# Half of the first expert's first layer moved into the first batch's attention, with new due times

## The chip, the cores and the metric

The kernel runs on one core of a Trainium2 chip. The metric is the device time of one execution in microseconds, as a median over runs. The engines are TensorE (PE; its weight loads have a row of their own, PEld), VectorE (DVE), ScalarE (ACT), GpSimd (POOL) and SyncE (SP), which here only issues DMAs. Each engine works through its own queue in order and waits on semaphores for the others.

## The reference

Attention over pooled queries, then two feed-forward networks, everything in fp32. B = 2 batches, H = 8 heads, 1152 keys, 576 pooled queries, head size 64; the model width is 512.

```python
q_pool = q.reshape(B, H, S // 2, 2, D).mean(axis=3)
scores = q_pool @ k.T / sqrt(D)
attn = exp(scores - max(scores)); attn = attn / (attn.sum() + 1e-9)
x = (attn @ v), as [1152, 512]
p = domain_probs / (domain_probs.sum(-1) + 1e-9)
out = sum over 4 experts e of p[:, e] * (relu(x @ w1[e]) @ w2[e])      # 512 -> 1024 -> 512
g = out @ w_gate
result = (g * sigmoid(g) * (out @ w_val)) @ w_out                      # 512 -> 1536 -> 512
```

## The kernel before, in words

**Attention** is cut into 32 units u: batch, pair of heads, half of the queries (288 of them), head within the pair. Units 0 to 15 are batch 0, 16 to 31 batch 1. A unit has nine chunks of 128 keys. Its steps are: `scores` (two chunks into one pair of PSUM banks, two products of 128x288 for each chunk, L503 and L504), `copy_scores` (ACT, L520, the bank into the SBUF tile `s`), `max_scores` (DVE, L527 to L531, a running maximum `acc`), `turn_max` (PE transposes `acc`, tile `mt`, L537), `reduce_max` (DVE, `top`, L547), `spread_max` (PE, `m`, L559), `copy_max` (ACT, L569), `subtract` (three groups of three chunks, L576: group 0 on DVE, groups 1 and 2 on POOL), `expo` (ACT, L582), `av` (PE, L609, the product with the values), `take_part`, `invert`, `scale` (ACT, DVE, POOL: numerator over denominator into `xst`) and `split_x` (L360, L363). Transposes of keys and queries (`prep_k`, `prep_q`, tile `tr`, L447 and L473) stand between them. In batch 0 `av` is an fp32 product, which takes two PE instructions; nearly everything else splits an fp32 number into a high and a low half and makes three products (hi·hi, hi·lo, lo·hi) in their place. In batch 1 the exponentials are split too (`half_hi`, `half_lo`, L587 and L594).

**PSUM** in this part has three pairs of banks p0, p1, p2 and two single banks c and d. Scores go round p0, p1, p2. Bank c holds the `av` sums. All transposes, `mt` and `m` share bank d, so each of them waits until the one before has been read.

**Experts** (`experts`, L873): for each batch and expert eight column blocks f of layer 1, each a sum over four 128-row chunks c of x (chunk c holds heads 2c and 2c+1) for both halves s of the queries, 24 matmuls of 128x288; then layer 2, also 192 matmuls. Blocks go to p0 and p1 in turn; `evict_h` (ACT, L914) and `evict_h2` (DVE, L918) empty one. Weights come in pieces of 256 KB (`load_piece`, three buffers) and are split by `split_hi` (ACT, L315) and `split_lo` (L322; for batch 0's odd pieces POOL, else DVE). Batch 0's experts run between the steps of batch 1's attention, batch 1's experts after it, and then the gated network (tile `g`, then `o`).

**Order.** Nobody writes the order of attention and batch 0's experts by hand. Each step is given to a planner with a due time, an engine, a cost and the names that it reads, writes and holds (`at`). `Plan.arrange` then goes through the engines and on each picks, of the steps that are ready, the one with the earliest due time. So a table of due times sets every queue's order, and on the chip the queues then run as fast as their waits allow. Unit u's steps are due at 9u plus a number for each kind of step; the experts' products are due at

```python
total = experts(0, at, lambda n: E0_START + n / E0_RATE)
```

with n a count of matmuls.

Of the kernel before, what the change touches and what calls it, by code (L numbers as in the profile page):

```python
# [21 lines left out]
TOP = (1.875 - 2.0**-23) * 2.0**-96  # L22
# [4 lines left out]
MT, TOP, MB, MCOPY = 10.23, 11.11, 11.18, 12.05  # L27
SUB = (11.07, 10.75, 13.58)
EXP = ((13.43, 16.94, 15.82), (12.68, 14.5, 17.57))
HALF_HI = (14.41, 16.21, 16.25)  # L30
HALF_LO = (13.1, 15.0, 17.1)
AV = (17.93, 15.5)
FINISH = (22.33, 24.2)
SHARE = (0.7, 2.54, 2.4, 3.2, 3.7)
COPY, MAX = 0.94, 0.25
PREP_Q, PREP_K = (4.3, 5.58, 0.4), (6.33, -0.27)
SPLIT = (-9.69, -6)
E0_START = 159.71
E0_RATE = 9.69
LAST = 18  # L40
# [123 lines left out]
def tile_kernel(  # L164
# [14 lines left out]
    P = 128  # L179
# [72 lines left out]
    def columns(w, c0, c1, o):  # L252
        return w[c0 * P : c1 * P, o * P : (o + 1) * P].rearrange("(c p) o -> p c o", p=P)
# [31 lines left out]
    def narrow(i, words):  # L285
# [6 lines left out]
            up, words[:, :, 1].bitcast(F32), DOWN, TOP, op0=ALU.mult, op1=ALU.min  # L292
        )
        nc.vector.tensor_scalar_max(up, up, -TOP)
# [211 lines left out]
    def score_bank(u, c):  # L506
        return "p2" if u >= LAST else f"p{(u * (KC + 1) // 2 + c // 2) % 3}"
# [137 lines left out]
    def plan_attention():  # L645
        def due_k(jj, g, t, bank):
# [5 lines left out]
            for i in range(2):  # L652
                at(
                    t + PREP_K[1], "ACT", 0.48, prep_k_half, jj, g, i, False,
                    reads=[("ptk", jj, g)], writes=[("kth", jj, i, g)],
# [3 lines left out]
                    t + PREP_K[1], "DVE", 0.555, prep_k_half, jj, g, i, True,  # L659
# [4 lines left out]
        def due_q(u, t, bank):  # L664
# [6 lines left out]
                t + PREP_Q[2], "ACT", 0.41, prep_q_hi, u,  # L671
# [3 lines left out]
                t + PREP_Q[2], "DVE", 0.45, prep_q_lo, u,  # L675
# [31 lines left out]
        for u in range(B * UPB):  # L707
            t = KC * u
            b, jj, half, i = where(u)
            r = 2 * half + i  # L710
            for c in range(0, KC, 2):
# [11 lines left out]
                    t + c + COPY, "ACT", 0.65 if n == 2 else 0.41, copy_scores, u, c,  # L723
                    reads=[("sc", u, c)],
                    writes=[("s", u, c + m) for m in range(n)],
                    **{"uses" if c else "takes": [("S", u) if c else ("s", ("S", u))]},
                )
                if c:
                    at(
                        t + c + MAX, "DVE", 0.75 if n == 2 else 0.92,  # L730
# [7 lines left out]
                t + MT, "PE", 0.25, turn_max, u, kind="f",  # L738
# [3 lines left out]
                t + TOP, "DVE", 0.555, reduce_max, u,  # L742
# [3 lines left out]
                t + MB, "PE", 0.2, spread_max, u, kind="f",  # L746
# [3 lines left out]
                t + MCOPY, "ACT", 0.41, copy_max, u,  # L750
                reads=[("m", u)], writes=[("mc", u)], takes=[("m", ("mc", u))],
            )
            for g in range(3):
                chunks = range(3 * g, 3 * g + 3)
                at(
                    t + SUB[g], "POOL" if g else "DVE", 2.05 if g else 1.05, subtract, u, g,
# [5 lines left out]
                    t + EXP[b][g], "ACT", 0.925, expo, u, g,  # L762
                    writes=[("s", u, c) for c in chunks], uses=[("S", u)],
                )
                if b:
                    at(
                        t + HALF_HI[g], "ACT", 0.925, half_hi, u, g,
# [4 lines left out]
                        t + HALF_LO[g], "POOL" if g else "DVE", 2.05 if g else 1.05, half_lo, u, g,  # L772
# [6 lines left out]
                for cs in [chunks] if b == 0 else [[c] for c in chunks]:  # L779
                    at(  # L780
                        t + AV[b] + cs[0], "PE", 1.46 if b == 0 else 0.397, av, u, cs,
# [8 lines left out]
            end = t + FINISH[b]  # L790
            p = u // 2
            for n in range(2):
# [3 lines left out]
                    reads=[("av", u)], writes=[(tag, p, i)], takes=[] if i else [(tag, (tag, p, 2))],  # L796
                    uses=[(tag, p, 2)],
                )
            if i == 1:
                for n in range(2):  # L800
                    at(
                        end + SHARE[n], "DVE", 1.02, invert, u, n,
# [4 lines left out]
                    end + SHARE[2], "POOL", 0.85, scale, u, kind="port",  # L807
# [76 lines left out]

    def experts(b, at, due):

        pbs, hs, pss, yts = {}, {}, {}, {}
        n = 0
        w = b * PER_BATCH

# [301 lines left out]
```

## Time and profile before

| | |
|---|---|
| time, three runs | median 919.43 us (918.15 to 921.57) |
| the profiled execution | span 920.0 us from the first instruction to the last; the page gives it no other time |
| PE busy, PEld busy | 890.4 us (97%), 845.9 us (92%) |
| DVE, ACT, POOL busy | 575.9, 462.0, 387.7 us |
| chain that ended last | 87% PE |

A row of the profile's stretches has, for each engine, its busy time in that stretch and the count of its instructions. PE counts a matmul as busy from its issue to its modelled end, so that several overlap; PEld counts weight loads, one for each matmul. PEclk is the clock that TensorE was granted, as a share of 2.4 GHz; 0.50 is 1.2 GHz.

### The profile page before, as it was taken

To read this page: it belongs to the slowest core of one execution; us is meant where nothing else is said; L and a number is where in the kernel's file an instruction comes from. 1 tells how busy PE (TensorE), PEld (TensorE's weight loads), DVE (VectorE), ACT (ScalarE), POOL (GpSimd) and SP (SyncE) were. 2 spreads that over 40 slices of the span, in tenths; PEclk is the share of its full clock that TensorE was granted. 3 is DMA by queue.
4 is the path that set the end of the run, shared out by engine and by line. 5 is a ranking of instruction groups with operands and counts; after the bars stand their busy time and mean duration, and the time that the engine had idled before them with its cause. 6 is when DMAs were issued, how large, how long until landed. Compare 5 with 4: busy or idle time off the path is not lost.

```text
span 920.0 us, 14980 instructions
## 1 busy us (share of the span) xinstructions
PE 890.4 (97%) x5916; PEld 845.9 (92%) x5916; DVE 575.9 (63%) x883; ACT 462.0 (50%) x786; POOL 387.7 (42%) x266
## 2 busy tenths in 40 slices
PE   5898989999999999999999999999999999999998
PEld 4777767899999999999999999999999999999886
DVE  5678877766667577675654334333468988888800
ACT  5678868877777677666633223232323333333110
POOL 4456566767776796778631000203023332222000
PEclk9999999999999999999999999999999999999999
DMA  5031121323233223112243232323333322223210
GB/s 141 1 78 39 41 74 51 87 73 86 66 89 87 70 73 83 46 59 60 58 149 94 87 100 81 94 83 89 94 93 96 111 69 92 92 75 101 78 69 34
DMA packets 124149, 72.30 MB, mean 79 GB/s; under 512 B 32304, under 2 KB 119344, under 8 KB 124080
## 3 DMA queue, kind: packets, MB, share of 16 engines
q1 hardware_dynamic: 124080, 71.36, 26.8%
q8 instruction: 46, 0.75, 0.3%
q14 instruction: 23, 0.19, 0.1%
HBM read 68.96 MB, written 2.38 MB: 78 GB/s over the span
## 4 chain that ended last, share of the span: by engine, by line
PE 87%; DVE 5%; ACT 4%; POOL 2%; issue 2%; DMA 0%; SPq 0%; DVEq 0%; POOLq 0%; ACTq 0%
PE ps L873 43%; PE g L873 16%; PE av L609 11%; PE o L873 8%; PE sc L503 3%; PE sc L504 3%; DVE acc L531 1%; ACT s L520 1%; POOL s L576 1%; ACT s L582 1%; PE mt L537 1%; PE tr L447 1%; PE tr L473 1%; ACT kt L463 1%; DVE kt L465 1%
## 5 line engine op out<-in xcount | busy, mean ns | idle before, releaser
L315 ACT ACTIVATE whi<-wraw 128x512 fp32r<-128x512 f32 x128 | 80.6, 630 | 172.5 <-PE ps L873 153.8
L576 POOL TENSOR_TENSOR s<-s,m 128x864 f32<-128x864 f32 x64 | 132.1, 2084 | 78.5 <-ACT m L569 78.4
L873 PE MATMUL ps<-xhi,whi 128*128 128x288 f32 x512 | 153.0, 299 | 0.0
L873 PE MATMUL ps<-hhi,whi 128*128 128x288 f32 x512 | 152.2, 297 | 0.0
L873 PE MATMUL ps<-hhi,wlo 128*128 128x288 f32 x512 | 151.0, 295 | 0.0
L873 PE MATMUL ps<-xhi,wlo 128*128 128x288 f32 x512 | 151.0, 295 | 0.0
L873 PE MATMUL ps<-hlo,whi 128*128 128x288 f32 x512 | 150.9, 295 | 0.0
L873 PE MATMUL ps<-xlo,whi 128*128 128x288 f32 x512 | 150.9, 295 | 0.0
L322 DVE TENSOR_TENSOR wlo<-wraw,whi 128x512 fp32r<-128x512 f32 x96 | 80.2, 835 | 102.1 <-ACT whi L315 101.9
L940 POOL TENSOR_TENSOR yacc<-yacc,yt 128x576 f32<-128x576 f32 x24 | 41.3, 1723 | 187.8 <-DVE yt L934 187.8
L520 ACT ACTIVATE s<-sc 128x576 f32<-128x576 f32 (+1 forms) x160 | 93.2, 601 | 52.2 <-PE sc L504 50.7
L582 ACT ACTIVATE s<-s 128x864 f32<-128x864 f32 x96 | 87.6, 920 | 20.0 <-DVE s L576 15.0
L873 PE MATMUL g<-yhi,wlo 128*128 128x384 f32 x288 | 96.3, 334 | 0.5 <-DVE wlo L322 0.5
L873 PE MATMUL g<-yhi,whi 128*128 128x384 f32 x288 | 96.2, 334 | 0.5 <-ACT yhi L1031 0.5
L873 PE MATMUL g<-ylo,whi 128*128 128x384 f32 x288 | 96.2, 334 | 0.0
L873 PEld LDWEIGHTS ps<-xlo,whi 128*128 128x128 f32 x512 | 96.2, 188 | 0.0
L873 PEld LDWEIGHTS ps<-hlo,whi 128*128 128x128 f32 x512 | 96.1, 188 | 0.0
L873 PEld LDWEIGHTS ps<-xhi,whi 128*128 128x128 f32 x512 | 96.1, 188 | 0.0
L873 PEld LDWEIGHTS ps<-hhi,whi 128*128 128x128 f32 x512 | 96.1, 188 | 0.0
L873 PEld LDWEIGHTS ps<-xhi,wlo 128*128 128x128 f32 x512 | 96.1, 188 | 0.0
L873 PEld LDWEIGHTS ps<-hhi,wlo 128*128 128x128 f32 x512 | 96.1, 188 | 0.0
L503 PE MATMUL sc<-qhi,kt 128*128 128x288 f32 x288 | 88.8, 324 | 5.9 <-DVE acc L531 2.8
(94 smaller groups left out, 1957.8 us busy)
## 6 DMA issues: line engine op xcount, KB each, us to landing
wraw<-in_moe_w_dram SPq DMA_DIRECT2D x128, 256.0 KB, 2.7
w<-in_moe_w_gate_dram SPq DMA_DIRECT2D x12, 512.0 KB, 3.7
w<-in_moe_w_val_dram SPq DMA_DIRECT2D x12, 512.0 KB, 3.7
w<-in_moe_w_out_dram SPq DMA_DIRECT2D x12, 512.0 KB, 3.5
qraw<-in_q_dram SPq DMA_DIRECT2D x32, 144.0 KB, 2.3
kraw<-in_k_dram SPq DMA_DIRECT2D x14, 288.0 KB, 3.7
v<-in_v_dram SPq DMA_DIRECT2D x8, 288.0 KB, 4.0
vraw<-in_v_dram SPq DMA_DIRECT2D x8, 288.0 KB, 3.0
```

What stands on the lines that cost most here:

```text
L315: nc.scalar.activation(out=hi, in_=t, func=AF.Copy)
L322: eng.tensor_tensor(out=lo, in0=t, in1=hi.bitcast(F32), op=ALU.subtract)
L447: nc.tensor.matmul(pt[:, m * P : (m + 1) * P], kr[:, c].rearrange("p h d -> p (h d)"), ident, is_transpose=True,)
L463: nc.scalar.activation(out=kt[me, sl], in_=pt[me, : 3 * P], func=AF.Copy)
L503: nc.tensor.matmul(ps, wt, qhi, start=True, stop=False)
L504: nc.tensor.matmul(ps, wt, qlo, start=False, stop=True)
L520: nc.scalar.activation(out=s[:, c : c + n, :], in_=ps[:, :n, :W], func=AF.Copy)
L576: eng.tensor_tensor(out=sg, in0=sg, in1=m.unsqueeze(1).to_broadcast([P, 3, W]), op=ALU.subtract)
L582: nc.scalar.activation(out=sg, in_=sg, func=AF.Exp)
L609: nc.tensor.matmul(avs[u][:, :W], w[:, c].rearrange("p t d -> p (t d)"), e, start=(c == 0 and n == 0), stop=(c == KC - 1 and n == len(term ...
L873: nc.tensor.matmul(ps, w, x, start=first and n == 0, stop=last and n == len(terms) - 1)
L940: nc.gpsimd.tensor_tensor(out=y, in0=y, in1=yts[o], op=ALU.add)
```

## The change

For expert 0 of batch 0 layer 1 is made in two parts. **Early part**: chunks c = 0 and 1 of x, heads 0 to 3, 12 matmuls for each of the eight blocks, 96 in all. They are due from 96.12 on at 1.625 matmuls per unit of time, within batch 0's attention. They go to bank pair p1, and `evict_early` copies each block out as fp32 (even blocks ACT, odd ones DVE) into a tile that `hlo` will use later. From unit 8 on scores therefore use only p0 and p2. **Late part**: chunks 2 and 3, the other 96 matmuls, where the whole block stood; then `add_early` (DVE) adds the saved sum in PSUM, and `evict_h` and `evict_h2` follow as before. The weight pieces of this layer are cut anew: two chunks by two blocks, so that pieces 0 to 3 serve the early part and 4 to 7 the late one; their number and size stay. Three of these are loaded about 54 units of time sooner.

The due times become a table `DUE` with three numbers for each kind of step: units 0 to 7, units 8 to 15, and batch 1. Three extra dependencies keep the planner's bookkeeping right. `TOP` is renamed to `LIMIT` where it is a number (that code runs for other input types only).

```diff
...
-MT, TOP, MB, MCOPY = 10.23, 11.11, 11.18, 12.05
-COPY, MAX = 0.94, 0.25
...
+DUE = {
+    "mt": (4.55, 8.38, 4.08),
...
+    "copy": (-0.74, -7.74, -2.17),
...
+SPLIT = (0.43, 2.72)
+EARLY_SPLIT = (4.47, 17.53)
+E0_START = 161.44
+E0_RATE = 10.078
+E00_START = 96.12
+E00_RATE = 1.625
+EARLY = 8
+LAST = 17
...
-    for _ in range(B):
+    for b in range(B):
         for e in range(NE):
-            pieces += [columns(w1[e], 0, MC, f) for f in range(FC1)]
+            if b or e:
+                pieces += [columns(w1[e], 0, MC, f) for f in range(FC1)]
+            else:
+                for c in range(0, MC, 2):
+                    pieces += [columns(w1[e], c, c + 2, f, 2) for f in range(0, FC1, 2)]
             for o in range(MC):
...
     def score_bank(u, c):
-        return "p2" if u >= LAST else f"p{(u * (KC + 1) // 2 + c // 2) % 3}"
+        n = u * (KC + 1) // 2 + c // 2
+        return "p2" if u >= LAST else f"p{n % 2 * 2}" if u >= EARLY else f"p{n % 3}"
...
+        def during(u):
+            phase = 2 if u >= UPB else u // (UPB // 2)
+            return {name: times[phase] for name, times in DUE.items()}
...
+        def evict_early(f):
+            early[f] = hp.tile([P, SQ], F32, tag="hlo", name=f"part{f}")
+            out, ps = two(early[f]), pss[0, f, "early"][:, :, :W]
+            if f % 2:
+                nc.vector.tensor_copy(out=out, in_=ps)
+            else:
+                nc.scalar.activation(out=out, in_=ps, func=AF.Copy)
+
+        def add_early(f):
+            ps = pss[0, f][:, :, :W]
+            nc.vector.tensor_tensor(out=ps, in0=ps, in1=two(early[f]), op=ALU.add)
 
...
         def expert_bank(group):
-            return f"p{(group[0] * (FC1 + MC) + group[1]) % 2}"
+            return "p1" if len(group) == 3 else f"p{(group[0] * (FC1 + MC) + group[1]) % 2}"
...
+        if b == 0:
+            m = 0
+            for f in range(FC1):
+                group = (0, f, "early")
+                ps = ("ps", b, *group)
+                for s in range(NH):
+                    for c in range(2):
+                        hidden_product(
+                            due_early(m), group, ps, w, c, f % 2 * P, s, c, c == 0, c == 1
+                        )
+                        m += 3
+                    if f % 2 == 0 and s == 1:
+                        due_split(w + 1, due_early(m) + EARLY_SPLIT[0], due_early(m) + EARLY_SPLIT[1])
+                at(
+                    due_early(m - 1) + 0.1, ("ACT", "DVE")[f % 2], (0.64, 0.755)[f % 2],
+                    evict_early, f,
+                    reads=[(*ps, 0), (*ps, 1)], writes=[("part", f)], uses=[ps],
+                    takes=[("hlo", ("part", f))],
+                )
+                w += f % 2
+
...
+                late = b == 0 and e == 0 and hidden
+                    for c in range(2, MC) if late else range(MC):
+                        if late:
+                            hidden_product(
+                                due(n), group, ps, w, c - 2, f % 2 * P, s, c, c == 2, c == MC - 1
+                            )
...
+                    if s == (1 if late else 0) and not (late and f % 2):
+                        due_split(w + 1, due(n) + SPLIT[0], due(n) + SPLIT[1])
+                w += f % 2 if late else 1
+                if late:
+                    at(
+                        due(n - 1) + 0.3, "DVE", 0.76, add_early, f,
+                        reads=[("part", f)], writes=[(*ps, 0), (*ps, 1)], uses=[ps],
+                    )
...
         for n in range(3):
-            due_load(n, 130 + n)
-        due_split(0, E0_START - 4, E0_START - 3)
+            due_load(n, E00_START - 20 + n)
```

The order of the queues, before and after, at three places. First PE's queue where unit 0's maximum has been spread (tile m) and its exponentials are awaited; sc are scores, tr transposes of queries (qraw) or keys (kraw), av the products with the values. Before:

```order
L559 MATMUL m<-ident,top_235 128x96 x3
L473 MATMUL tr<-ident,qraw_96 128x96 x3
L609 MATMUL av<-s_176,v_102 128x288 x3
L473 MATMUL tr<-ident,qraw_96 128x96 x3
L503 MATMUL sc<-qhi_263,kt_131 128x288
L504 MATMUL sc<-qlo_270,kt_131 128x288
```

Now the row of m is followed by twelve score matmuls of unit 2, one transposition of queries and four more score matmuls of unit 2; the last two of these stand first here:

```order
L538 MATMUL sc<-qhi_212,kt_131 128x288
L539 MATMUL sc<-qlo_214,kt_131 128x288
L645 MATMUL av<-s_176,v_102 128x288 x3
L482 MATMUL tr<-ident,kraw_157 128x128 x3
L645 MATMUL av<-s_176,v_102 128x288 x6
L573 MATMUL mt<-ident,acc_235 96x128 x3
```

Sixteen score matmuls of unit 2 now stand ahead of unit 0's first av, where there were none; the other transposition of queries has gone ahead of unit 1's scores.

Second, PE's queue behind unit 10's m, two thirds through batch 0. Before:

```order
L609 MATMUL av<-s_883,v_104 128x288 x3
L537 MATMUL mt<-ident,acc_1013 96x128 x3
L609 MATMUL av<-s_883,v_104 128x288 x3
L559 MATMUL m<-ident,top_1117 128x96 x3
L503 MATMUL sc<-qhi_967,kt_652 128x288
L504 MATMUL sc<-qlo_974,kt_652 128x288
L473 MATMUL tr<-ident,qraw_964 128x96 x3
L609 MATMUL av<-s_980,v_102 128x288 x6
L473 MATMUL tr<-ident,qraw_964 128x96 x3
```

Now (m stands six rows ahead of the first one here, with a group of av and two chunks' scores between; ps<-xhi and so on are early products, of which twelve follow in a row up to the second transposition):

```order
L538 MATMUL sc<-qhi_993,kt_649 128x288
L539 MATMUL sc<-qlo_1003,kt_649 128x288
L645 MATMUL av<-s_908,v_104 128x288 x3
L508 MATMUL tr<-ident,qraw_990 128x96 x3
L918 MATMUL ps<-xhi_496,whi_869 128x288
L918 MATMUL ps<-xlo_497,whi_869 128x288
L918 MATMUL ps<-xhi_496,wlo_870 128x288
```

Between m and the transposition of queries, where one chunk's scores stood, there are now three chunks' scores and two groups of av, and behind it early products.

Third, DVE's queue where the first expert starts (hlo is `evict_h2`, el `half_lo`, s `subtract`, acc the maximum, den the denominator, wlo `split_lo`, top `reduce_max`). Before:

```order
L531 TENSOR_TENSOR acc_1826<-sc,s_1766 128x576
L322 TENSOR_TENSOR wlo_1829<-wraw_1304,whi_1828 128x512
L918 SCALAR_TENSOR_TENSOR hlo<-ps,hhi 128x576 x2
L576 TENSOR_TENSOR s_1614<-s_1614,m 128x864
L531 TENSOR_TENSOR acc_1826<-sc,acc_1826 128x576
L626 TENSOR_SCALAR den_1899<-av 64x288
L594 TENSOR_TENSOR el_0_1929<-s_1614,eh_0_1902 128x864
L918 SCALAR_TENSOR_TENSOR hlo<-ps,hhi 128x576
```

Now (the rows ps<-ps,part are `add_early`):

```order
L969 TENSOR_TENSOR ps<-ps,part_1071 128x2x288
L583 TENSOR_REDUCE top_1927<-mt 96x3
L969 TENSOR_TENSOR ps<-ps,part_1145 128x2x288
L978 SCALAR_TENSOR_TENSOR hlo<-ps,hhi 128x576
L612 TENSOR_TENSOR s_1770<-s_1770,m 128x864
L567 TENSOR_TENSOR acc_1971<-sc,s_1941 128x576
L978 SCALAR_TENSOR_TENSOR hlo<-ps,hhi 128x576
L969 TENSOR_TENSOR ps<-ps,part_1209 128x2x288
L357 TENSOR_TENSOR wlo_1915<-wraw_1593,whi_1914 128x512
L978 SCALAR_TENSOR_TENSOR hlo<-ps,hhi 128x576
L969 TENSOR_TENSOR ps<-ps,part_1375 128x2x288
L662 TENSOR_SCALAR den_2037<-av 64x288
```

Each block's row hlo now has an addition ahead of it, and the blocks follow each other after 12 matmuls instead of 24.

Three counts from PE's whole queue. When unit 15's last av had been issued, all scores of unit 17 had been too; now those of five of its nine chunks stand behind it. From there to expert 0's last layer-1 matmul there now stand 96 late products, 36 score matmuls, 48 av matmuls, and transposes of q, mt and m. Behind unit 31's last av there stood 150 matmuls of expert 3 before batch 1's first product; now there are 48.

## Rows read from the trace of the kernel before

**Rows 1.** The page: busy time by engine, its share of the span, instructions.

```profile
PE 890.4 (97%) x5916; PEld 845.9 (92%) x5916; DVE 575.9 (63%) x883; ACT 462.0 (50%) x786; POOL 387.7 (42%) x266
```

**Rows 2.** Stretches: length, busy time (count) of each engine, PEclk, DMA share, GB/s.

```profile
24.00:26.00 2.00, 2.00 (x8) 1.46 (x7) 0.00 (x0) 0.40 (x2) 0.89 (x2) 0.50 0.04 8
...
120.00:122.00 2.00, 2.00 (x6) 1.41 (x5) 0.63 (x2) 1.26 (x2) 1.39 (x3) 0.50 0.00 0
...
28.00:176.00 148.00, 133.60 (x734) 106.35 (x734) 114.30 (x187) 114.97 (x205) 87.89 (x64) 0.99 0.21 54
100.00:176.00 76.00, 68.69 (x371) 54.53 (x370) 59.61 (x100) 59.09 (x107) 46.97 (x37) 0.98 0.26 69
...
176.00:488.00 312.00, 311.64 (x2385) 310.79 (x2384) 206.94 (x272) 209.34 (x340) 219.37 (x136) 1.00 0.27 77
...
520.00:560.00 40.00, 40.00 (x304) 40.00 (x303) 15.32 (x23) 10.97 (x19) 0.00 (x0) 1.00 0.29 88
```

**Rows 3.** Timeline of PE: start, duration, instructions (idle before them, and its releaser).

```profile
18.45 0.46 PE L559 MATMUL m<-ident,top 96*128 96x96 f32 x3
21.32 0.71 PE L473 MATMUL tr<-ident,qraw 96*128 96x96 f32 x3 [2.40 <-issue]
22.23 3.25 PE L609 MATMUL av<-s,v 128*128 128x288 f32 x6 [0.20 <-ACT s L582]
...
115.90 0.29 PE L504 MATMUL sc<-qlo,kt 128*128 128x288 f32 x1
117.72 0.44 PE L473 MATMUL tr<-ident,qraw 96*128 96x96 f32 x3 [1.53 <-issue]
118.63 4.87 PE L609 MATMUL av<-s,v 128*128 128x288 f32 x12 [0.47 <-ACT s L582]
...
172.05 4.56 PE L609 MATMUL av<-s,v 128*128 128x288 f32 x18
176.44 0.41 PE L473 MATMUL tr<-ident,qraw 96*128 96x96 f32 x3
176.64 0.38 PE L873 MATMUL ps<-xhi,whi 128*128 128x288 f32 x1
```

**Rows 4.** The chain that ended last, 28 to 180: start, duration, what.

```profile
39.38 1.46 PE av L609 x6
```

**Rows 5.** Waits from 28 to 176: who for whom, total us, times, longest.

```profile
PE sc L503 <- DVE acc L531: 2.1, 6, 0.5
```

**Rows 6.** DVE's groups by line, 176 to 488: count, busy us, mean ns.

```profile
L322 DVE TENSOR_TENSOR wlo<-wraw,whi 128x512 fp32r<-128x512 f32 x32 | 36.0, 1125 | 16.4 <-ACT whi L315 16.3
L594 DVE TENSOR_TENSOR el<-s,eh 128x864 fp32r<-128x864 f32 x16 | 25.5, 1594 | 9.2 <-ACT eh L587 8.9
L918 DVE SCALAR_TENSOR_TENSOR hlo<-ps,hhi 128x576 fp32r<-128x576 f32 x32 | 24.0, 750 | 11.3 <-ACT hhi L914 11.1
L531 DVE TENSOR_TENSOR acc<-sc,acc 128x576 f32<-128x576 f32 x28 | 20.9, 745 | 4.7 <-ACT s L520 4.4
L633 DVE RECIPROCAL den<-den 128x144 f32<-128x144 f32 x18 | 18.6, 1042 | 0.3
L576 DVE TENSOR_TENSOR s<-s,m 128x864 f32<-128x864 f32 x15 | 15.7, 1046 | 2.2 <-ACT m L569 2.2
```

**Rows 7.** ACT's groups by line, 176 to 488.

```profile
L315 ACT ACTIVATE whi<-wraw 128x512 fp32r<-128x512 f32 x64 | 40.2, 628 | 40.2 <-PE ps L873 21.5 <-issue 12.5 <-POOL xst L641 2.5
L520 ACT ACTIVATE s<-sc 128x576 f32<-128x576 f32 x56 | 36.4, 650 | 36.2 <-PE sc L504 35.9
L914 ACT ACTIVATE hhi<-ps 128x576 fp32r<-128x576 f32 x32 | 20.5, 639 | 0.2
```

**Rows 8.** Timeline, all engines, behind unit 31's last value product; then batch 1's first product.

```profile
467.64 0.30 PE L609 MATMUL av<-el,vh 128*128 128x288 f32 x1
...
474.00 0.75 DVE L363 TENSOR_TENSOR xlo<-xst,xhi 128x576 fp32r<-128x576 f32 x1
...
487.66 0.29 PE L873 MATMUL ps<-xhi,whi 128*128 128x288 f32 x1
```

More of the change, by code (lines that the diff above doesn't have):

```diff
@@ L722, in plan_attention @@
                 at(
-                    t + c + COPY, "ACT", 0.65 if n == 2 else 0.41, copy_scores, u, c,
-                    reads=[("sc", u, c)],
-                    writes=[("s", u, c + m) for m in range(n)],
+                    t + c + due["copy"], "ACT", 0.65 if n == 2 else 0.41, copy_scores, u, c,
+                    reads=[("sc", u, c)] + ([("opened", u)] if c else []),
+                    writes=[("s", u, c + m) for m in range(n)] + ([] if c else [("opened", u)]),
                     **{"uses" if c else "takes": [("S", u) if c else ("s", ("S", u))]},
@@ L755, in plan_attention @@
                 at(
-                    t + SUB[g], "POOL" if g else "DVE", 2.05 if g else 1.05, subtract, u, g,
+                    t + due[f"sub{g}"], "POOL" if g else "DVE", 2.05 if g else 1.05, subtract, u, g,
                     kind="port" if g else None,
@@ L771, in plan_attention @@
                     at(
-                        t + HALF_LO[g], "POOL" if g else "DVE", 2.05 if g else 1.05, half_lo, u, g,
+                        t + due[f"lo{g}"], "POOL" if g else "DVE", 2.05 if g else 1.05, half_lo, u, g,
                         kind="port",
@@ L789, in plan_attention @@
                     )
-            end = t + FINISH[b]
+            end = t + due["finish"]
             p = u // 2
@@ L806, in plan_attention @@
                 at(
-                    end + SHARE[2], "POOL", 0.85, scale, u, kind="port",
+                    end + due["scale"], "POOL", 0.85, scale, u, kind="port",
                     reads=[("num", p, 0), ("num", p, 1), ("den", p, 0), ("den", p, 1)],
@@ L895, in load_p, with products @@
             )
-        def products(group, i, s, c, src, first, last):
+        def products(group, i, at_c, at_o, s, src, first, last):
             if group not in pss:
                 pss[group] = pair(expert_bank(group), "ps")
-            whi, wlo = (h[:, c, :] for h in halves[i])
+            whi, wlo = (h[:, at_c, at_o : at_o + P] for h in halves[i])
             xhi, xlo = (x[:, subs[s]] for x in src())
@@ L940, in add_y, with due_product, hidden_product @@
             nc.gpsimd.tensor_tensor(out=y, in0=y, in1=yts[o], op=ALU.add)
+        def due_product(t, group, ps, i, at_c, at_o, s, src, reads, uses, first, last, opens):
+            at(
+                t, "PE", 0.397, products, group, i, at_c, at_o, s, src, first, last,
+                kind="r", reads=reads + [("whi", i), ("wlo", i)],
+                writes=[(*ps, s)] + ([(*ps, 1)] if opens else []),
+                uses=uses + [ps],
+                takes=[(expert_bank(group), ps)] if opens else [],
+            )
+        def hidden_product(t, group, ps, i, at_c, at_o, s, c, first, last):
+            half = s if b == 0 else 0
+            due_product(
+                t, group, ps, i, at_c, at_o, s, lambda: [x[:, c, :] for x in xts[b]],
+                [("xhi", b, c, half), ("xlo", b, c, half)], [("x", b)], first, last,
+                first and s == 0,
+            )
[19 more added lines that the diff above has]
+                w += f % 2
         for e in range(NE):
```

138 lines of the change are left out of this document (78 added, 60 removed).

## Prediction

> **What bounds the kernel now.** I read the page first, then the stretches, then PE's timeline. The page has PE busy for 97% of the span [rows 1], which seems to leave nothing to win by moving matmuls. The stretches say where that is not so. From 176 to 488 and from 520 to 560 PE is full by any measure: 40 us hold 304 matmuls, one each 131.6 ns, and the weight loads, one for each matmul, fill 310.79 of 312 us [rows 2]. There the end moves by what PE has left to do, and by nothing else. From 28 to 176, batch 0's attention, matmul rows still cover 133.6 of 148 us, but weight loads only 106.35 [rows 2]. Since weight loads reach 100% where PE is full, they are the better gauge: 41.7 us of 148 are open. The other engines are not full either: ACT 115.0, DVE 114.3, POOL 87.9 of 148 [rows 2]. So that stretch is held by the chain through four engines, not by one of them, and matmuls from the full stretch can go into its openings if their operands are there. I predict the time by this: how much work PE has behind it when the full stretch begins, and when that is.
>
> The Trainium skill, page Perfetto Trace Analysis, section Identifying the Most-Contended Engine, says that matmul busy time is a poor measure of TensorE's headroom and that the busy share of weight loads is a fair one. By matmul rows, 100 to 176 has only 7.3 us open, so at least 4 of the 11.3 us that come in below would push the attention back, and the sum would be 913.7 us; the trace agrees with the page in that weight loads, and not matmul rows, tell the two stretches apart. The sum below needs neither.
>
> **The change, part by part.** The sum is made against the profiled execution's 920.0 us, 0.6 above the median of the runs.
>
> *Moved matmuls.* 96 early products at 131.6 ns leave the full stretch: 12.6 us. At the point where PE ends unit 15's av (176.4 in the trace, with the first expert product at 176.64 [rows 3]), the old order had all of unit 17's scores behind it; in the new one five of their chunks, ten matmuls, are still to come: 1.3 us. If that point stays at 176.4, the gain is 11.3 us.
>
> *Head of batch 0.* PE sits idle for 2.4 us ahead of 21.32, waiting for bank d, which the subtraction still reads, and then runs at 1.2 GHz (clock 0.50): six av take 3.25 us in place of 1.46 [rows 2 to 4]. The six score matmuls that follow before the clock is back lose up to their 131.6 ns each, an estimate. The hole costs PE 2.4 + 1.8 + 0.8 = 5.0 us. The new queue has sixteen score matmuls there, 2.1 us. They need banks that the maximum gives back, so not all of them run at once. Bounds 0 and 5; I take half, 2.5 us, as a later start of the next units is what counts, and part of that is caught up in the chain anyway.
>
> *Second half of batch 0.* Costs: PE takes 11.3 us more. In 100 to 176, where most of it falls, weight loads then cover 54.5 + 11.3 = 65.8 of 76 us, 87%. ACT gets four copies out (nearest row 639 ns) and about three weight splits (628 ns), 4.4 us, to 63.5 of 76; DVE four copies (nearest row 745 ns) and two more splits (1125 ns with POOL at work), 5.2 us, to 64.8 of 76 [rows 2, 6, 7]. Three engines at 84 to 87% in one chain will not hide everything. Gain: the hole at 115.9, where PE waits 1.53 us for bank d and then makes twelve av in 4.87 instead of 2.92 us at 1.2 GHz [rows 2, 3], is filled by two chunks' more scores and two groups of av, and twelve early products stand right behind. Bounds: a loss of 12.6 us if each early product pushes the attention by its length, a gain of 3.5 us if all hide and the hole goes. With each of the three engines still 10 us short of full, I am nearer to the good end: a loss of 3 us, a quarter of what was moved.
>
> *DVE at the start of the experts.* Late blocks come every 12 matmuls, 1.6 us, and each needs an addition (745 ns as the nearest row), `evict_h` (639) and `evict_h2` (750) before its bank is free [rows 6, 7]. From unit 15's last av to expert 0's last layer-1 matmul the new PE queue holds 96 late products (12.6 us), 36 score matmuls (4.7), 48 av matmuls (6.3) and some 1.5 us of small transposes: 25 us. DVE's queue for the same work holds, by these rows, 8 additions (6.0), 8 `evict_h2` (6.0), the maxima of 18 chunks (6.3), two el at 1594 ns (3.2), two wlo at 1125 ns (2.3), two reciprocals (2.1), two subtractions (2.1) and seven shorter instructions, some 3 us: 31 us. So DVE is 6 us too slow here. Layer 2's first piece, 24 matmuls or 3.2 us, does not need the last block and hides part. The old order had twice the matmuls for each `evict_h2`. Bounds 0 and 6; I take a loss of 3.5 us.
>
> *End of batch 1's attention.* Behind unit 31's last av there were 150 expert matmuls, 467.64 to 487.66, and x for batch 1 was whole at 474.75, 7.1 us after [rows 8]. In the new queue 48 stand there, 6.3 us, and nine of batch 1's own that need only the first three chunks, 1.2 us: 7.5 us of cover over 7.1 us. Loss 0, at worst 1. If that cover were gone, the 7.1 us would show in full.
>
> *Costs of nothing.* The additions, copies and splits of ACT and POOL in the full stretch lie beside PE (POOL 219 of 312 busy [rows 2]); if PE were not full there they would cost what DVE's do. The early weight pieces are the same bytes, loaded sooner, with DMA at 0.26 of its time [rows 2]. Behind 488 us nothing is moved.
>
> Sum: 12.6 − 1.3 + 2.5 − 3.0 − 3.5 − 0 = 7.3 us, 912.7 on the profiled execution, 912 on the median's scale.
>
> **Rivals.**
>
> *The attention gives it all back* (no change). The chain through bank d, ACT and DVE sets batch 0's pace, and each early product that PE takes up stands ahead of some link. For it: PE's waits are short and for many releasers, so openings are small pieces; the longest that PE's scores wait for DVE's maximum are six times 2.1 us in all [rows 5]. Against it: two large holes, 115.9 and 18.9 [rows 3]. Price: the second half costs 9 instead of 3 us, time 918.
>
> *Two banks for scores* (slower). From unit 8 on scores go to p0 and p2 in turn. A pair of chunks holds its bank for its own 0.53 us (four times 131.6 ns), the copy (650 ns) and the maximum (745 ns) [rows 2, 6, 7], at least 1.9 us in line, and PE's queue stops at the next but one if that is not done. Now the third bank covers this, and PE has waited for the maximum only six times, 2.1 us in all [rows 5]. With two, five such starts a unit, and 0.4 us of wait at each (what each of those six cost: 0.35), nine units lose 18 us; less the 10.3 us that the rest of the sum brings without the second half's 3 us: 928. It decides from 0.23 us a start on. Against it: five pairs at 1.9 us on two banks fill only 4.8 us of a unit's 9 to 10 (148 us hold some 16 units), and the new due times spread the pairs between av and products.
> The Trainium skill, page Perfetto Trace Analysis, section Matmuls, advises that independent groups rotate through different PSUM banks so that emptying one overlaps the next; taking one of three away goes against it, and the six waits agree that the rotation just suffices now. It stands behind this rival and gives no number.
>
> *The due times do more* (much faster). Batch 0's pace tightens in both halves, holes go and nothing is pushed: 12.6 − 1.3 + 4 + 2 − 2 = 15.3 us, 904 on the median's scale.
>
> **Chances.** The forecast, 907 to 914.8, 0.54; the attention gives it back, 914.8 to 921, 0.21; two banks, 0.12; due times do more, 0.13. The range leaves out the tail of the slower rival and little of the good one: 904 to 920. What a measurement of this kernel can tell from no change is about 0.5%, 4.6 us: faster by more than that 0.67, within it 0.21, slower 0.12.
>
> **What would show it.** In the changed profile unit 15's last av should end at 174 to 179; later than 184 speaks for the second or third step's bad end, and waits of PE's scores for `copy_scores` or the maximum, many times those of now, for the two-bank rival. The clock should stay at 1.00 around 120. Between that point and some 30 us later PE should show waits for `evict_h2`, 2 to 5 us in all. From then to 488 less the gain, PE full; batch 1's first product without a wait. The stretch behind it should take the 432 us that it takes now; if it doesn't, something is wrong that I have not seen.

## The result, and the profile of the changed kernel

The changed kernel takes 912.82 us (median of 4 runs, 912.6 to 913.23), the kernel before 919.88 on the same chip; the ratio is 0.9915, 95% interval 0.9897 to 0.9933. The forecast was 912.0 in a range of 904 to 920. By the medians the gain is 7.1 us; the profiled execution has a span of 911.5 us against 920.0, a gain of 8.5.

The page of the changed kernel, busy time by engine, answers to [rows 1]:

```profile
PE 886.3 (97%) x5916; PEld 843.7 (93%) x5916; DVE 590.0 (65%) x895; ACT 463.9 (51%) x790; POOL 388.3 (43%) x266
```

The number of matmuls is the same, and the number of DVE's instructions has grown by 12 (eight additions, four copies). The stretches tell more. First those of the kernel before, in cuts that were not shown yet, then the changed kernel (columns as in [rows 2], which has 100 to 176 of the kernel before):

```profile
0.00:100.00 100.00, 82.89 (x444) 67.12 (x445) 67.59 (x110) 71.13 (x125) 52.14 (x46) 0.97 0.25 60
...
176.00:215.00 39.00, 38.64 (x299) 38.28 (x297) 26.27 (x37) 30.91 (x52) 28.89 (x20) 1.00 0.23 67
215.00:480.00 265.00, 265.00 (x2029) 264.51 (x2028) 178.18 (x232) 176.37 (x285) 187.80 (x115) 1.00 0.27 77
```

```profile
0.00:100.00 100.00, 87.23 (x481) 71.52 (x482) 72.02 (x117) 75.33 (x136) 55.97 (x50) 1.00 0.31 79
100.00:176.00 76.00, 72.42 (x439) 61.96 (x438) 63.19 (x99) 58.72 (x105) 47.34 (x36) 1.00 0.21 58
176.00:215.00 39.00, 35.96 (x265) 34.36 (x264) 35.87 (x48) 32.24 (x52) 29.27 (x20) 1.00 0.16 51
215.00:480.00 265.00, 263.99 (x2019) 262.85 (x2018) 175.40 (x230) 175.62 (x283) 186.31 (x114) 1.00 0.26 74
```

The granted clock, 0.97 and 0.98 up to 176 us before, is now 1.00 throughout. The first bracket is the count of PE's matmuls, and it makes a ledger: at 131.6 ns each, the lead of the changed kernel over the one before. It is 37 at 100 us and 105 at 176 (481 + 439 against 444 + 371), 13.8 us; 34 of them are lost between 176 and 215, where PE is no longer full, and 10 more to 480. What stays is 61, or 8.0 us, against the 8.5 of the span. So it is neither a pure gain nor a small one: 13.8 us are won and 5.8 are given back.

PE's timeline of the changed kernel at the end of unit 15's last av, at the same anchor as in [rows 3], then batch 1's first product with what goes before it, which answers to [rows 8]; the second fence is DVE's timeline:

```profile
172.41 1.65 PE L645 MATMUL av<-s,v 128*128 128x288 f32 x6
173.68 0.51 PE L538 MATMUL sc<-qhi,kt 128*128 128x288 f32 x1
...
479.04 0.30 PE L918 MATMUL ps<-hhi,wlo 128*128 128x288 f32 x1
479.18 0.29 PE L918 MATMUL ps<-xhi,whi 128*128 128x288 f32 x1
...
480.36 0.30 PE L918 MATMUL ps<-xhi,whi 128*128 128x288 f32 x1
```

```profile
478.99 0.74 DVE L398 TENSOR_TENSOR xlo<-xst,xhi 128x576 fp32r<-128x576 f32 x1
```

Unit 15's end, taken here and below as the start of PE's next row, comes 2.8 us earlier (173.7 against 176.4; the prediction had 174 to 179). Batch 1 begins 8.5 us earlier (479.18 against 487.66) with no idle time ahead of it, though x became whole only at 479.73; the product that needs it came at 480.36. The stretch from there to the end is 432.3 us in both.

PE's waits in the changed kernel from 173 to 215 (who, for whom, total us, times, longest):

```profile
PE ps L918 <- DVE hlo L978: 1.3, 1, 1.3
PE sc L538 <- DVE acc L567: 0.8, 2, 0.4
PE mt L573 <- DVE acc L564: 0.7, 1, 0.7
PE av L645 <- DVE el L630: 0.2, 1, 0.2
```

The longest wait is for `evict_h2`: 1.3 us, where the prediction had 2 to 5. Here is why it was late, on DVE's and then on POOL's timeline of the changed kernel:

```profile
186.92 0.75 DVE L978 SCALAR_TENSOR_TENSOR hlo<-ps,hhi 128x576 fp32r<-128x576 f32 x1
187.58 0.76 DVE L969 TENSOR_TENSOR ps<-ps,part 128x576 f32<-128x576 f32 x1
188.25 3.07 DVE L357 TENSOR_TENSOR wlo<-wraw,whi 128x512 fp32r<-128x512 f32 x1
191.25 0.74 DVE L978 SCALAR_TENSOR_TENSOR hlo<-ps,hhi 128x576 fp32r<-128x576 f32 x1
```

```profile
186.69 4.08 POOL L612 TENSOR_TENSOR s<-s,m 128x864 f32<-128x864 f32 x2
```

While POOL makes two subtractions, DVE's instructions with an operand in PSUM pass in 0.75 us, and the one whose two operands both lie in SBUF (`wlo`, 0.68 us where POOL is idle) ends only when POOL has ended both. This is not in the prediction, and it comes back in several of the experiments.

### The profile page after: what moved, and what is told of

It reads as the page before. It is cut to its first block, busy times and chain, and to the rows that moved or that the text cites. A ratio compares the mean times of both kernels' runs of the same rounds, so it can differ in the third digit from the quotient of the medians.

```text
span 911.5 us, 14995 instructions
## 1 busy us (share of the span) xinstructions
PE 886.3 (97%) x5916; PEld 843.7 (93%) x5916; DVE 590.0 (65%) x895; ACT 463.9 (51%) x790; POOL 388.3 (43%) x266
## 4 chain that ended last, share of the span: by engine, by line
PE 87%; DVE 6%; ACT 3%; issue 2%; POOL 1%; DMA 0%; SPq 0%; DVEq 0%; POOLq 0%; ACTq 0%
PE ps L918 41%; PE g L918 16%; PE av L645 12%; PE o L918 8%; PE sc L538 4%; PE sc L539 3%; DVE acc L567 1%; ACT s L556 1%; PE mt L573 1%; PE tr L482 1%; DVE wlo L357 1%; PE tr L508 1%; ACT kt L498 1%; PE m L595 1%; DVE kt L500 1%
## 5 line engine op out<-in xcount | busy, mean ns | idle before, releaser
L357 DVE TENSOR_TENSOR wlo<-wraw,whi 128x512 fp32r<-128x512 f32 x96 | 84.6, 881 | 92.3 <-ACT whi L350 92.3
```

The source lines that it names most:

```text
L357: eng.tensor_tensor(out=lo, in0=t, in1=hi.bitcast(F32), op=ALU.subtract)
```

## The experiments

Every run is given by its median and its ratio to the kernel before, whose median was 920.4 to 920.8 in each set of runs. The changed kernel itself stands at 0.9915. Diffs are against the changed kernel, unless they say otherwise. Where an edit keeps "its own order", the planner lists the same work as before and only what is issued at its places differs, so that every other instruction stands where it stood. The interval of a ratio reaches 1 to 1.8 us to either side, so a difference below 2 us between two edited kernels rests on their traces as well.

**Each half of the change alone.** The early part with the old table:

```
+OLD = {
+    "mt": 10.23, "top": 11.11, "mb": 11.18, "mcopy": 12.05,
...
+    "k0": 6.33, "k1": 6.33, "k2": 6.33, "v": 6.7, "khalf": -0.27,
+}
+DUE = {name: (time,) * 3 for name, time in OLD.items()}
...
```

> The early part as in the changed kernel, but with the old due times of the attention in all three phases; the two banks for scores, the unit from which scores have one bank, and the due times of the expert products stay as changed. Theory: the moved matmuls bring their 12.6 us whatever the table, but only the table fills the two holes of batch 0 (clock at half speed near 20 us and near 120 us). So unit 15's last av ends at 178 to 184 in place of 173.7, and the time is 917 to 923, 4 to 10 us above the changed kernel. Rival (the early products fill the openings of the old order by themselves): the end of unit 15 at 174 to 177, the time 913 to 916.

940.21 us, ratio 1.0221 (1.0200 to 1.0241): far outside what both theories allowed. In the old order the two banks for scores alone cost 6 to 8 of these 20 us (the last experiment). The new table without the early part:

```
-late = b == 0 and e == 0 and hidden
+late = False
-        if b == 0:
+        if False:
             m = 0
...
-EARLY = 8
-LAST = 17
+EARLY = 99
+LAST = 18
```

(the pieces of the weights, the start and rate of the expert products and the lead of their splits are those of before).

> The new due times of the attention alone: all of expert 0's layer 1 at its old place, weights in the old pieces, scores on three banks to the unit where they were, expert due times as before. Theory: the head of batch 0 gains its 4 us and the hole near 120 us goes, while no early product stands in the way, so unit 15's last av ends at 169 to 173 and the time is 913 to 916.5, 3.5 to 7 us below the kernel before. Rival 1 (the new table is only there to make room for the early products and is worth nothing alone): 918.5 to 921. Rival 2 (the table does all): 912 to 913.

929.43 us, 1.0095 (1.0082 to 1.0109), slower than the kernel before, which no theory had. With the two kernels they make a square: old table and no early part 919.9, early part alone 940.2, table alone 929.4, both 912.8. (The start and rate of the expert products, the splits and the banks go with the early part in this square.) The effects do not add; each is a loss without the other.

Both traces show where. With the table alone, PE is 31 matmuls ahead of the kernel before at 176 us, 4.1 us, so the head does gain by the table by itself. Then it loses 66 in 39 us (the windows of that run from 176 to 215, PE's first row behind the longest wait, then its DVE and its POOL):

```profile
176.00:215.00 39.00, 33.32 (x233) 32.87 (x233) 26.56 (x31) 26.30 (x43) 26.27 (x18) 0.91 0.19 58
...
191.73 0.58 PE L918 MATMUL ps<-xhi,whi 128*128 128x288 f32 x1 [5.62 <-DVE hlo L978]
```

```profile
185.62 5.29 DVE L357 TENSOR_TENSOR wlo<-wraw,whi 128x512 fp32r<-128x512 f32 x1 [0.58 <-ACT whi L350]
190.84 1.41 DVE L978 SCALAR_TENSOR_TENSOR hlo<-ps,hhi 128x576 fp32r<-128x576 f32 x2
```

```profile
185.14 2.03 POOL L612 TENSOR_TENSOR s<-s,m 128x864 f32<-128x864 f32 x1
187.13 1.26 POOL L357 TENSOR_TENSOR wlo<-wraw,whi 128x512 fp32r<-128x512 f32 x1
188.35 2.01 POOL L612 TENSOR_TENSOR s<-s,m 128x864 f32<-128x864 f32 x1
```

One weight subtraction stood on DVE through three instructions of POOL, `evict_h2` behind it, and PE behind that, for 5.62 us; then the clock was granted at half for some 6 us (0.91 over the window). With the early part alone, unit 15 ends at 183.9, 7.4 us later than before, and PE, full in the changed kernel, is open at the end of batch 0's experts (that run's windows; 304 matmuls would fill the second):

```profile
215.00:480.00 265.00, 258.54 (x1967) 256.04 (x1965) 175.98 (x229) 175.15 (x285) 186.68 (x112) 1.00 0.24 70
480.00:520.00 40.00, 36.00 (x245) 34.71 (x244) 21.98 (x26) 14.37 (x23) 13.69 (x9) 0.91 0.35 107
```

There the last av matmul begins at 495.93, batch 1's first product at 499.34, and x is whole at 506.58. The old times of batch 1's attention, beside products that come sooner, would do this; no run takes them apart.

**That collision taken away** (against the run with the table alone, in its own order):

```
-eng = nc.gpsimd if i < PER_BATCH and i % 2 else nc.vector
+eng = nc.gpsimd if i < PER_BATCH and (i % 2 or i == 2) else nc.vector
```

> The run with the new due times alone, in its own order, but with the low half of one weight piece, the third, made on POOL in place of DVE. In that run DVE's subtraction for it began at 185.6 and took 5.29 us, until POOL had done three instructions, evict_h2 stood behind it, PE waited 5.8 us for that and then ran 26 matmuls at half clock. Theory (that one collision makes most of what the new due times alone lose): the hole falls below 1.5 us and the time is 920 to 924. Rival (the order itself is bad and another wait takes its place): 927 to 930.

926.23 us, 1.0057 (1.0041 to 1.0073). The hole went: 270 matmuls from 176 to 215 in place of 233. But the time fell by 3.2 us, where the 5.62 us of wait and the half clock behind it had cost 8.4, and lies above the theory's range, since 7 of those 37 matmuls had been lost before 176 and batch 1's stretch stayed as open as it was (2001 matmuls to 480, against 2029). The collision is shown as the cause of the hole, not of all that the table loses alone.

**Is a matmul taken from the full stretch worth 131.6 ns?** The kernel before in its own order, with 96 products left out:

```
 def products(group, i, s, c, src, first, last):
+    if b == 0 and group[0] == 0 and group[1] < FC1:
+        if c < 2:
+            return
+        first = c == 2
```

> The kernel before in its own order, in which the products of the first two chunks of expert 0's layer 1 in batch 0 are not issued: 96 matmuls less behind unit 15, and nothing put anywhere else; the result lacks the first four heads there. Theory (PE is full there, a matmul taken away is 131.6 ns off the end): 12.6 us less, 906.5 to 909. Rival (half blocks bring evict_h2 and the banks into the chain, or x of batch 1 loses its cover): 910 to 915.

918.12 us, 0.9980 (0.9970 to 0.9989): 2.4 us of 12.6, less than even the rival had. The windows of that run show that the place stays open (x222, where the kernel before has 299):

```profile
176.00:215.00 39.00, 30.13 (x222) 28.18 (x221) 30.34 (x42) 32.46 (x55) 29.18 (x21) 1.00 0.31 87
```

PE's order there alternates products with the steps of units 16 and 17, and without the products it stood at those steps: its waits in the window, 8.9 us, are for the query halves (3.6), el (1.6), the maximum (1.4), the key halves (1.1), and the weight halves (1.2), and none is for `evict_h2`, which the rival named. A fixed order can't fill the place, so the same work was left out of the planner's list too:

```
-for c in range(MC):
+for c in range(2 if short else 0, MC):
...
-    due_split(w + 1, due(n + SPLIT[0]), due(n + SPLIT[1]))
+    off = (-5, -4) if short else SPLIT
+    due_split(w + 1, due(n + off[0]), due(n + off[1]))
```

> The kernel before without the first two chunks of expert 0's layer 1 in batch 0, which the planner does not know either, so all expert work behind them is due 96 products earlier and the queue is written anew (the shorter blocks' weight pieces are split some 5 products later in them than before); the result lacks the first four heads there. Theory (the 12.6 us come once the planner pulls later products into the place): PE's waits between 176 and 215 stay below 5 us and the time is 907 to 911. Rival (units 16 and 17 need that much cover whatever stands there): waits of 8 us or more and 912 to 918.

920.42 us, 0.9993 (0.9984 to 1.0002), outside both ranges. With 12.6 us of PE's work gone, nothing is gained. Its trace has the losses one by one. The windows, then DVE's timeline:

```profile
176.00:215.00 39.00, 32.67 (x226) 30.90 (x225) 28.07 (x33) 25.86 (x45) 23.75 (x17) 0.91 0.27 78
...
480.00:520.00 40.00, 38.18 (x273) 37.51 (x272) 20.41 (x29) 13.21 (x22) 6.16 (x4) 0.96 0.39 120
```

```profile
187.42 5.01 DVE L322 TENSOR_TENSOR wlo<-wraw,whi 128x512 fp32r<-128x512 f32 x1
192.35 1.41 DVE L918 SCALAR_TENSOR_TENSOR hlo<-ps,hhi 128x576 fp32r<-128x576 f32 x2
```

73 matmuls (9.6 us) less from 176 to 215 than in the kernel before, the larger part at a collision of the same kind (PE waited 5.1 us for `evict_h2`, again with half the clock behind). And 31 (4.1 us) less from 480 on: x of batch 1 was whole at 486.24, its first product came at 484.54. In the kernel before, 150 products stood behind unit 31's last av [rows 8]; here it was 7.3 us of them, and x was whole 9.0 us after it. The splits of the shorter blocks were moved too (`SPLIT` is -9.69 and -6), and what that does to the collision alone was not run; the second loss lies far from them.

**What the early products push.** The changed kernel in its own order, with early products, their copies and the additions not issued:

```
 def products(group, i, at_c, at_o, s, src, first, last):
+    if len(group) == 3:
+        return
...
 def evict_early(f):
+    return
...
 def add_early(f):
+    return
```

> The changed kernel in its own order, in which the 96 early products, the eight copies of their sums and the eight additions are not issued; the result lacks the first four heads in expert 0's layer 1. All else, weights of the early pieces too, stands where it stood. Theory of the prediction (three engines at 84 to 87% hide most but not all): unit 15's last av ends at 169.5 to 172 in place of 173.9, and the additions give 1.5 us more behind it; the time is 907 to 909. Rival 1 (early products lie wholly in openings): unit 15 ends at 173 to 174 and the time is 910.5 to 911.5, that of the run without additions. Rival 2 (each pushes by its own length): unit 15 ends at 161 to 163, the time is 897 to 900.

909.25 us, 0.9885 (0.9869 to 0.9900). Unit 15 ends at 171.6, 2.1 us earlier than with 96 early products, 12.6 us, among its work. But the profiled execution was the longest of the four (910.91 against 909.14 to 909.34), and its clock fell to half ahead of all early products, where the changed kernel's did not. The same six av in this run, then in the changed kernel:

```profile
77.17 3.18 PE L645 MATMUL av<-s,v 128*128 128x288 f32 x6 [0.30 <-ACT s L618]
...
77.48 1.72 PE L645 MATMUL av<-s,v 128*128 128x288 f32 x6 [0.30 <-ACT s L618]
```

Behind this dip PE's other matmuls have lost 1.7 us against the changed kernel, so without it the 2.1 would be up to 3.8. By the medians, 2.2 us lie between this run and the next one, which keeps the early products. So some 9 to 10.5 of 12.6 us lie in openings that this order has anyway. That is what the prediction's theory said, though the time lies 0.25 us above its range; both rivals are out.

**What the additions cost.**

```
-                if late:
-                    at(
-                        due(n - 1) + 0.3, "DVE", 0.76, add_early, f,
-                        reads=[("part", f)], writes=[(*ps, 0), (*ps, 1)], uses=[ps],
-                    )
```

> The changed kernel without the eight additions: the early sums are made and copied out, but never added, so the result lacks the products of the first four heads in expert 0's layer 1. Theory (DVE has too much to do at the start of the experts): eight additions of some 0.71 us, 5.7 us, leave DVE between 174 and 212, PE's waits there fall from some 5.5 us to 2 or less, and the time is 908.5 to 910.5. Rival (the waits there come from unit 17's scores, which have one bank, and from the chain through the transposes, not from DVE's load): 912 to 913.

911.45 us, 0.9899 (0.9884 to 0.9914); batch 1's first product comes 1.6 us earlier (477.56). DVE's busy time from 176 to 215 fell from 35.87 to 29.51 us, and of the 34 matmuls that PE lacks there only 8 came back:

```profile
176.00:215.00 39.00, 36.69 (x273) 35.30 (x272) 29.51 (x41) 32.25 (x54) 31.91 (x21) 1.00 0.20 58
```

So neither theory holds: the additions' 6 us of DVE are worth 1.4 to 1.6 us.

**Other causes of the waits behind unit 15.** Unit 17's scores on two banks:

```
-LAST = 17
+LAST = 18
```

> The changed kernel with unit 17's scores on two banks in turn, as for the units before it; from unit 18 on they have one. Theory (of 5.5 us of waits between 173 and 212 some 2 us are unit 17's scores, which wait for the maximum on the one bank, and the transposed maximum that comes late with them): 910.5 to 912. Rival (unit 17 then shares a bank with the late blocks, which wait in its place): 913 to 916.

912.49 us, 0.9911 (0.9896 to 0.9926): between the theories, and no different from the changed kernel. Its window from 176 to 215 has 268 matmuls, 3 more, with other waits in place of the old ones (1.1 us for `evict_h2`, 0.7 for el). Two collisions of DVE and POOL taken away, in the changed kernel's own order:

```
-at(100, "SP", 0.5, load_probs, writes=[("praw",)])
-at(104, "DVE", 1.5, prep_probs, reads=[("praw",)], writes=[("pn",)])
+load_probs()
+at(100, "SP", 0.5, lambda: None, writes=[("praw",)])
+at(104, "DVE", 1.5, lambda: None, reads=[("praw",)], writes=[("pn",)])
...
             nc.vector.tensor_tensor(out=a, in0=ps[:, :, :W], in1=other, op=ALU.max)
+            if (u, c) == (7, 2):
+                prep_probs()
...
-eng = nc.gpsimd if i < PER_BATCH and i % 2 else nc.vector
+eng = nc.gpsimd if i < PER_BATCH and (i % 2 or i == 6) else nc.vector
```

> The changed kernel in its own order, with two collisions of DVE and POOL taken away: DVE normalises the probabilities some 36 us earlier, while POOL has nothing to do (now one of these short instructions takes 2.08 us at 106.8), and the low half of the seventh weight piece is made on POOL (now DVE takes 3.07 us for it at 188.3, evict_h2 stands behind it, PE waits 1.5 us). Theory (waits at the start of the experts come from such collisions as much as from DVE's load): PE's wait at 190.5 goes and so does 1 us or more before 176; the time is 909.5 to 911.5. Rival (POOL's queue only moves the wait to the second subtraction of unit 17): 912.5 to 914.

914.69 us, 0.9932 (0.9920 to 0.9945), slower, as the rival had it and by more, though at another instruction. Unit 15 ends at 171.1, 2.6 us earlier. But with one more piece, POOL worked from 182.5 to 192.6 nearly without a pause, and the next DVE instruction with two operands in SBUF stood longer than the one that was removed. DVE's timeline of that run, and PE's longest wait:

```profile
188.90 4.64 DVE L632 TENSOR_TENSOR el<-s,eh 128x864 fp32r<-128x864 f32 x1
```

```profile
PE av L647 <- DVE el L632: 3.7, 2, 3.5
```

With the first of the two edits alone:

> The changed kernel in its own order, with nothing but the normalising of the probabilities moved: DVE does it some 36 us earlier, while POOL has nothing to do. Theory (a short DVE instruction behind POOL's subtraction at 106.8 makes two waits of PE before 120, 1.5 and 1.8 us; without it unit 15's last av ends at 171.3, and the collisions behind stay about as they are in the changed kernel): 909.5 to 911. Rival (what is gained before 176 is given back at the start of the experts, as in the run with the piece on POOL): 912 to 913.5.

912.02 us, 0.9903 (0.9890 to 0.9917), in the rival's range by its number and not to be told from the changed kernel. But what the rival says doesn't show: the window from 176 to 215 has 265 matmuls, as in the changed kernel, so nothing won is given back there. The waits near 110 and 116 are gone here too, yet unit 15 ends at 173.1: the clock fell to half near 78 us in that execution, and PE is 13 matmuls behind the changed kernel at 100 us (468, clock 0.98), where the run with both edits was not (479). Of the four executions the two with a clock of 0.998 took 912.69 and 912.75 us, the others 910.53 and 911.35, so the edit may be worth more without that dip. The collision at 187.67 is there as before (3.08 us).

**Two banks for scores, alone, in the kernel before.**

```
-        return "p2" if u >= LAST else f"p{(u * (KC + 1) // 2 + c // 2) % 3}"
+        n = u * (KC + 1) // 2 + c // 2
+        return "p2" if u >= LAST else f"p{n % 2 * 2}" if 8 <= u < 17 else f"p{n % 3}"
```

> The kernel before with nothing but the scores of units 8 to 16 on two banks in turn in place of three (and the order of a unit's first copy before its others kept by a dependence). Theory: five pairs a unit at 1.9 us of bank time each on two banks fit into a unit's 9 to 10 us, so the old order loses at most 0.2 us a unit, 919 to 922. The two-bank rival of the prediction: 0.4 us at each of five starts in nine units, 18 us, 930 to 938.

928.50 us, 1.0091 (1.0078 to 1.0105), which is neither. The trace has one large hole, PE behind bank d, with DVE and POOL on that run's timelines:

```profile
109.92 3.87 DVE L245 TENSOR_TENSOR pn<-praw,total 128x9 f32<-128x9 f32 x4
113.71 1.04 DVE L577 TENSOR_TENSOR s<-s,m 128x864 f32<-128x864 f32 x1
```

```profile
109.69 3.99 POOL L577 TENSOR_TENSOR s<-s,m 128x864 f32<-128x864 f32 x2 [2.33 <-ACT m L570]
```

```profile
114.81 0.90 PE L447 MATMUL tr<-ident,kraw 128*128 128x128 f32 x3 [4.64 <-DVE s L577]
```

Four multiplications of nine elements (0.40 us where POOL has just ended) took 3.87 us beside POOL's two subtractions. The same kernel with the seven short instructions elsewhere:

```
             nc.vector.tensor_scalar_add(t, avs[u][other, :W], EPS)
+            if u == 3:
+                prep_probs()
```

> The run with two banks for the scores of units 8 to 16 in the kernel before, every instruction at its place but the seven short ones that normalise the expert probabilities, which DVE now makes 47 us earlier, behind unit 3's denominators, while POOL has nothing to do (their load is issued at the start). Theory (the 8 us were not the banks: four multiplications of 9 elements stood behind POOL's subtractions for 3.87 us on DVE, held bank d, and PE had a hole of 4.8 us with half the clock behind it): the hole at 109.9 goes, the time is 919 to 922. Rival (the scores' two banks cost it): 926 to 929.

926.93 us, 1.0072 (1.0056 to 1.0088). The hole went and unit 15 ends 3.0 us earlier than in the run above (180.65 against 183.62), but still 4.2 us later than in the kernel before; by the medians 1.6 of 8 us came back, and the rival's number held. My theory falls: in the old order the two banks, or the order that the planner makes for them, do cost 4 us and more (6.4 by the medians), and the collision made the rest.

## Why the prediction was right, step by step

The time was right, and the sum came to it with two terms that were wrong, by 3.0 and 2.3 us in opposite directions, and one sentence that was wrong. That these two errors nearly cancel is luck.

*Moved matmuls, 12.6 us.* In the changed kernel they come through: all 96 early products, 9 ahead of 100 us and 87 behind it, are done before 176, where the lead is 105 matmuls. But the step that was to carry it, "there the end moves by what PE has left to do, and by nothing else", failed. Left out of the kernel before, the same products gave 2.4 us in the old order and nothing in a new one. A full PE said that no time was open, not that the work had nothing else to wait for: units 16 and 17 and batch 1's x were covered by just those products. The changed kernel covers x anew, and units 16 and 17 except for the loss told below. Which of the new numbers does it (the batch-1 times, the start and rate of the experts, unit 17's bank) was not taken apart; only that the old table doesn't is shown.

*Scores of unit 17 (−1.3), head (+2.5) and second half (−3.0)*, in all −1.8. Measured: 37 matmuls of lead at 100 us less 9 early products are 28, 3.7 us, for the head, near its upper bound of 5; unit 7's denominators come 4.9 us earlier, and the clock is 1.00 up to 176. From 100 to 176 there are 439 less 87 early ones, 352 against 371, a loss of 2.5 us, with unit 17's scores in it; the run without early products puts 2.1 us, and up to 3.8, on those. So in all +1.2. The head was mis-sized, since I halved it for banks that hardly held it up (the sixteen scores waited 0.60 us for the maximum); weight loads as the gauge of what can be hidden held, and the rival in which the attention gives all back is refuted by 9 to 10.5 us hidden of 12.6.

*DVE at the start of the experts, −3.5.* The size was 4.5 us by 215 and 5.8 by 480, and the cause was wrong in the main. I had counted DVE's busy time against PE's. Without the additions 26 of 34 lost matmuls stay lost, so the load is the smaller part. I had priced wlo at its mean of 1125 ns; in that stretch its three took 3.07, 1.12 and 2.12 us, against 0.68 without POOL, and what counts is which one has `evict_h2` or el behind it. The rest (unit 17's scores and its transposed maximum, 1.5 us of waits) did not change the time with another bank. What the whole of it consists of stays open.

*End of batch 1, 0.* Right, and by a margin of 0.6 us: x whole at 479.73, needed at 480.36. The replanned run shows the price of missing it, 4.1 us.

*Two banks.* In the changed kernel PE's scores waited 1.5 us from 28 to 176 for the maximum's line that [rows 5] shows with 2.1: four times in place of six. In the old order the same two banks cost 4.2 us by unit 15's end and 6.4 by the medians, not the 18 of the rival. *The due times do more:* not by themselves, where 93 matmuls, 12.2 us, are lost behind 176 and 4.1 won ahead of it.

The sum by the measured terms: 12.6 + 1.2 − 5.8 = 8.0 us, where I had 7.3.

## What to carry to other kernels

A busy engine tells where time can't be found, not what a piece of its work is worth: leave the work out, once in the old order and once replanned, before a move is priced by its length. In a planned queue the numbers fit one list of work; half of such a change is no half of its effect, and must be priced with the table that goes with it. In a stretch where DVE and POOL are both busy, look for short instructions that take several us, and at what is queued behind them.

## What the runs showed of the hardware

A DVE instruction that takes all its operands from SBUF waited while POOL worked; one operand in PSUM was enough to pass (0.75 and 0.76 us at 186.92 and 187.58, beside POOL's 4.08 us). How long it waited differed. In the collisions shown above it stood through several of POOL's instructions in a row: 5.29 us through three, 5.01 and 4.64 in the same way, 3.07 through two. Elsewhere, some ten times in the changed kernel up to 500 us, it got in when one of POOL's instructions ended, and POOL's next one took longer. One such case there, DVE and then POOL (two subtractions in 4.55 us, where the two at 186.69 took 4.08):

```profile
320.25 1.71 DVE L357 TENSOR_TENSOR wlo<-wraw,whi 128x512 fp32r<-128x512 f32 x1
```

```profile
319.32 4.55 POOL L612 TENSOR_TENSOR s<-s,m 128x864 f32<-128x864 f32 x2 [0.48 <-ACT m L605]
```

What decides which of the two goes next is open.

The Trainium skill, page SBUF — State Buffer, section Who interferes with whom, says that a DVE instruction with two SBUF inputs contends with a GpSimd instruction that reads SBUF, and that the shared port pair is an exclusive lock. The trace agrees on who waits and on who passes. The page also lets a `tensor_scalar` contend in its 2-port modes; in the changed kernel one of nine elements, from SBUF to SBUF, took 2.08 us beside POOL (0.17 without it, in the run with two banks), which agrees.

A hole of PE costs more than its length: after 5.62 us without a matmul 26 matmuls came 240 ns apart in place of 131.6, another 2.8 us (clock 0.91 over the 39 us).
